# The last chunk's blocks finished by VectorE's add and a plain store, a plain matmul for the biases, one more tile added in chunk 2

## The chip, the cores and the metric

The kernel runs on one core of a Trainium2 chip. The metric is device time in microseconds; before the change it is 209.16 (median of three runs, 208.89 to 209.57). One execution was profiled.

## The reference

One layer with two branches on the same normalized input, 2048 rows of 640, bf16:

```python
x = A_x
xn = _layernorm(x, axis=-1)
return x + _A_ref(xn, A_wqkv, A_wo) + _B_ref(xn, B_w1, B_b1, B_w2, B_b2)

# branch A: 32 heads of 20; row s attends to rows s, s-2, ..., s-14
qkv = (x @ wqkv).reshape(B, S, 3, H, Dh)            # then q, k, v by head
idx = pos[:, None] - (arange(8) * 2)[None, :]       # masked where idx < 0
logits = einsum("bhsd,bhswd->bhsw", q, kg) * scale  # kg, vg: k, v gathered at idx
o = einsum("bhsw,bhswd->bhsd", softmax(logits), vg)
A = o.reshape(B, S, D) @ wo

# branch B: a layer of 1536
B = einsum("bsf,fd->bsd", gelu(einsum("bsd,df->bsf", x, w1) + b1), w2) + b2
```

## The kernel before

The 2048 rows are cut into four chunks (0 to 3) of 512 rows, each of four blocks of 128. For a chunk: statistics and normalized rows (`st`, `su`, `sq`, `rs`, `rc`, `xn`), the transpose xnT (`tp` and `tc` on TensorE for chunk 0, a DMA transpose `tc` on the SP queue for the others), the projections q, k, v in five groups of five matmuls each (`pj`, copied from PSUM by ScalarE's `pc`; chunk 0 in halves, `hj` and `hc`), and the hidden layer in twelve groups of five (`f1`), with Gelu on ScalarE (`ge`).

The attention multiplies q by shifted k on VectorE (`qk`, into two large tiles `half[0]` and `half[1]`, four window positions each and five slices of 128 features). TensorE sums over features with a 128x32 matrix `head_of` (`lg`, line 483): per half one round of four matmuls (one for each block) for each slice. To make these fewer, VectorE first adds slices together: `pa` adds slices 1 and 3 onto 0 and 2, `pb` adds slice 2 and then 4 onto 0. `LEVEL[n]` says how far this goes in chunk n: 0 leaves five slices to TensorE, 1 leaves three, 2 two, 3 one. Then the softmax: maximum and subtraction (`m`, `mx`), exponential on ScalarE (`ex`), sums (`ss`), reciprocal on ScalarE (`ri`), product (`at`), an expansion of the weights by DMA (`xd`, `xs`, SP queue), products with v into the same `half` tiles (`av`), three adds (`ad`) and a last one into `oT` (`ot`, line 606). `oT` has one buffer for all chunks.

Output of chunks 0 to 2: for each slice s of 128 output features a PSUM tile T gathers five pieces `t{n}{s}0` to `4` (line 708): four of three matmuls over the hidden layer, and piece 4 of five matmuls over oT. ScalarE adds the bias (`u`), a DMA transpose on SP turns it back to rows (`ut`), and an accumulating DMA from POOL adds it in DRAM (`ud`) to x, which `xp` stored there earlier (SP for chunk 0, ScalarE's queue otherwise).

Output of chunk 3 is made by rows: `o3{bl}{pc}` has five pieces for each block bl, each of three (five) pairs of matmuls, `lo` for columns 0 to 511 and `hi` for 512 to 639. Blocks 12 and 13 (bl 0, 1) are copied from PSUM by ScalarE (`oc`) and accumulated by POOL (`od`) onto x (`xp3`) and the bias b2 (`xb3`, an accumulating DMA of the broadcast bias). Blocks 14 and 15 are direct: `xl` adds b2 to their x rows in SBUF, VectorE adds PSUM and x (`dc` for bl 2, `oclo` and `ochi` for bl 3, line 680) and plain stores write them (`dd`, the second half of `oclo`, `ochd`). The hi part of bl 3 comes last on TensorE (`ohi`, 17 matmuls of 128 columns). In PSUM bl 0 and the hi of bl 1 share the one place of pool psL; the hi parts of bl 2 and 3 share one place of psA.

PSUM pools: psA with four places (`pj`, `hj`, `f1`, the first transposes, and pieces of the last output), psL with one of twice the size (logits, the bias transpose, the last output), psO with two (T tiles, first transposes, lo of bl 3). A place is given again when the copy that empties it is done.

The biases b1 and b2 are loaded as 17 rows of 128 into `b_rt`; `tb` (line 460) transposes them on TensorE, in a 32x32 form, and `b1` copies them to `bT`.

The order of the work is one string, ORDER, written out by hand or by a search: the pieces are emitted in it, and each of TensorE, VectorE, ScalarE and the SP queue keeps this order as it stands; semaphores come from the data. So for each engine what stands ahead of a piece can be counted in the string.

Of the kernel before, what the change touches and what calls it, by code (L numbers as in the profile page):

```python
# [17 lines left out]
P = 128  # L18
# [11 lines left out]
LASTB = S // P - 1  # L30
DIRECT = 2
WARM = 10
RB = 32
# [3 lines left out]
LEVEL = (1, 0, 2, 3)  # L37
# [10 lines left out]
pc102 pa001 qk011 pj111 pc111 pj112 pj113 pc112 pa000 pa011 lg0 mask m0a mx0a ge0_4 pc113 ge0_10 ex0a pj103 pc103  # L48
pj104 pc104 ldx m0b mx0b ex0b ss0a ri0a pj110 pc110 ss0b ri0b pj114 pc114 pj100 pc100 ld2 pj101 at0a at0b xd0 pc101
qk110 qk100 su22 hj211 hc211 f10_1 pj121 su23 ge0_1 qk101 f10_6 qk111 ge0_6 f10_8 su21 ge0_8 su20 pc121 xs0 f10_9  # L50
# [5 lines left out]
av130 av100 t004 u00 ut00 sq31 pj200 pc200 t010 av101 t011 av120 t012 t013 t020 sq30 av131 t014 u01 ut01 sq33 f11_1  # L56
rs3 rc3 t021 t022 t023 t024 t030 t031 t032 t033 xn31 t034 tc31 ad10 pad21 xn33 tc33 ad11 pc203 ad12 ot1 ud00 f11_4
ud01 pc202 qk201 ge1_1 ge1_11 xn30 qk211 qk200 f11_8 f12_11 f12_9 qk210 pa211 tc30 pa200 pa210 xn32 tc32 pad22 ge1_8
ge2_9 pa201 f12_3 ge2_11 f11_6 ge1_6 ge1_4 f12_7 pad31 pb212 u02 pj320 pc320 ge2_7 pj304 pc304 pj311 pc311 pb202 pj313
pc313 pj312 pc312 pj222 u03 pc222 xl pj302 pc302 pj301 pj310 pj300 pc310 ge2_3 f13_2 pc300 pc301 pj314 pc314 pj322  # L60
pj303 pc303 pj321 lg2 f11_3 ge3_2 ge1_3 qk310 m2 ut02 f13_8 ge3_8 xb3 f12_5 pa301 t100 pc322 f13_6 t120 pj221 t101
t102 ge2_5 mx2 t121 f12_8 qk300 ex2 ss2 ri2 pa300 t103 pc221 ut03 ut04 ud02 at2 xd2 qk311 xs2 t104 ge2_8 f13_9 ge3_9
t122 t123 u10 f13_10 ge3_10 f13_7 ge3_7 qk301 ud03 pa311 pa310 f13_1 t110 ge3_1 ge3_6 t111 t112 t113 pj323 f12_1 pb302
pj223 pb312 pb304 pc223 pc321 ud04 pb314 t114 u11 pc323 ut10 ut11 f13_0 lg3 ud10 av200 t124 u12 t140 t141 m3 mx3 t130
t131 av210 ut12 t142 ex3 ss3 t143 pj324 av230 ri3 at3 t132 t133 t134 t144 ge3_0 av211 u13 av201 av220 f12_0 ge2_0
ge2_1 pc324 f13_4 ut13 f13_3 f12_4 av221 av231 ad20 ad21 u14 xd3 f13_5 ge2_4 ge3_3 ut14 o310 f12_6 ad22 ot2 ge3_5
ge3_4 o311 o312 ud11 ud12 ud13 ud14 f12_2 xs3 ge2_6 ge2_2 f12_10 pad32 ge2_10 o320 t210 t211 t212 t200 t201 t202
f13_11 ge3_11 t203 t204 t213 t214 u20 ut20 ud20 u21 ut21 ud21 av311 av301 t220 t221 t222 t230 av310 av321 o321 t223
t224 u22 ut22 ud22 t231 t232 t233 t234 u23 ut23 ud23 o330 o331 t240 t241 t242 o300 o301 o313 av330 av320 av300 av331
ad31 t243 t244 u24 ut24 ud24 ad30 o322 o323 ad32 ot3 o302 o303 o314 o304 o324 o332 dc dd o333 o334 ohi oclo ochi oc31  # L70
od31 oc30 ochd od30
# [4 lines left out]
def kernel(  # L76
# [37 lines left out]
    outp = ctx.enter_context(tc.tile_pool(name="outp", bufs=2))  # L114
# [7 lines left out]
    b_rt = consts.tile([RB, P], BF16, name="b_rt")  # L122
# [335 lines left out]
    def do_tb():  # L458
        tiles["tb"] = psL.tile([P, 2 * W * P], BF16, tag="L", name="tb")
        nc.tensor.transpose(tiles["tb"][:, 0:RB], b_rt[:], ident[0:RB, 0:RB])  # L460

    def do_b1():
        nc.vector.tensor_copy(bT[:], tiles["tb"][:, 0 : FT + KT])
# [171 lines left out]
    def out_ps(bl, hi):  # L635
        first = lambda: psL.tile([P, W, P], F32, tag="L", name="tail")
        if bl == 0 or (hi and bl == 1):
            ps = get("tail", first)[:].rearrange("p w c -> p (w c)")
            return ps[:, CH + bl * P : CH + (bl + 1) * P] if hi else ps[:, 0:CH]
        key = "hi" if hi else ("lo", bl)  # L640
        pool, tag = (psO, "o") if key == ("lo", BPC - 1) else (psA, "acc")
        ps = get(key, lambda: pool.tile([P, CH], F32, tag=tag, name="hi" if hi else "lo"))
        return ps[:, (bl - BPC + DIRECT) * P : (bl - BPC + DIRECT + 1) * P] if hi else ps[:]

    opened = set()

    def do_o(bl, pc, parts):
        n, cs = NCH - 1, slice(bl * P, (bl + 1) * P)
        if pc < 4:
            srcs = [(tiles["hT", n, ft][:, cs], w2_sb[:, ft, :]) for ft in range(3 * pc, 3 * pc + 3)]  # L650
        else:
            srcs = [(tiles["oT", n][:, t, cs], wo2[:, t, :]) for t in range(KT)]
        for k, (lhs, rhs) in enumerate(srcs):
            final = pc == 4 and k == len(srcs) - 1
            if "lo" in parts:
                nc.tensor.matmul(out_ps(bl, False), lhsT=lhs, rhs=rhs[:, 0:CH], start=pc == 0 and k == 0, stop=final)  # L656
            if "hi" in parts:
                bank = bl // 2
                first = bank not in opened
                opened.add(bank)  # L660
                nc.tensor.matmul(
                    out_ps(bl, True), lhsT=lhs, rhs=rhs[:, CH:D], start=first, stop=final, skip_group_check=True
                )
# [11 lines left out]
    def direct(bl, hi):  # L675

        b = (NCH - 1) * BPC + bl
        room = half[1][:].rearrange("p w t c -> p (w t c)")[:, (bl % 2) * D : (bl % 2 + 1) * D]
        cs = slice(CH, D) if hi else slice(0, CH)
        nc.vector.tensor_tensor(out=room[:, cs], in0=out_ps(bl, hi), in1=x_sb[:, b, cs], op=ALU.add)  # L680
        return room, out_sd[b * P : (b + 1) * P, :]
# [70 lines left out]
    for name in "tb b1 mean1 ho ldx ld2 ldo xl dc dd oclo ohi ochi ochd mask pk".split():  # L752
        piece(name, locals()[f"do_{name}"])
# [130 lines left out]
```

## Time and profile before

| | us |
|---|---|
| median of three runs | 209.16 (208.89 to 209.57) |
| the profiled execution, its time | 209.39 |
| its span | 207.2 |
| TensorE's last matmul ends | 203.8 |
| the last store lands | 205.99 |
| DMA transposes of xnT, issue to landing | 2.4 in the median, 5.7 at most |
| accumulating stores out_dram<-x_sb, issue to landing | 3.8 in the median |
| last stores out_dram<-half: 160 KB, 128 KB, 32 KB, issue to landing | 4.2, 2.2, 1.8 |

PE is TensorE, DVE VectorE, ACT ScalarE, SP the queue of the sync engine, POOL GpSimd. A timeline line has start and length, engine, line of the code, operation, output and input, shapes, count, and in brackets the idle time just before it and what ended it. Matmuls are pipelined: a row's length is that of one matmul from entry to exit, while the next one starts sooner. "Busy" of a group is the union of these lengths.

### The profile page before, as it was taken

Reading aid. Unit: us, or ns where it says so; the run is one execution under the profiler, and the core shown is the slowest. Engines: PE = TensorE matmul, PEld = TensorE weight load, DVE = VectorE, ACT = ScalarE, POOL = GpSimd, SP = SyncE. Lnnn points to the kernel's source line nnn. Section 1 sums busy time; section 2 is a strip of 40 time slices with the busy share of each in tenths; the row PEclk is TensorE's granted clock in tenths of the full one; section 3 lists DMA queues with packets and bytes.
Section 4 is the critical chain, followed back from the end, with each engine's and each line's share of the span. In section 5 each row is a group of like instructions: output and inputs, shape, how many; then the busy total and the mean of one; then the engine's idle time right before and its main releaser. Section 6 shows DMA issues by size and latency. Waiting matters only on the chain.

```text
span 207.2 us, 2936 instructions
## 1 busy us (share of the span) xinstructions
PE 201.7 (97%) x1137; PEld 106.8 (52%) x1156; DVE 182.6 (88%) x155; ACT 126.4 (61%) x232; POOL 23.9 (12%) x36
## 2 busy tenths in 40 slices
PE   8999999999999999999999999999999999999993
PEld 3999654644444555444455544444444444444552
DVE  2889994799799899999999989999899999999611
ACT  5778967999879877658685537571658621220120
POOL 2000000000000000420002400002040220224050
PEclk9999999999999999999999999999999999999999
DMA  6995879186063358479324800073472970285455
GB/s 211 389 395 180 60 209 394 39 187 209 0 186 67 130 118 211 103 99 86 69 27 52 75 3 0 0 156 73 53 69 45 157 110 3 51 76 51 54 37 115
DMA packets 36607, 23.56 MB, mean 114 GB/s; under 512 B 24946, under 2 KB 34418, under 8 KB 36594
## 3 DMA queue, kind: packets, MB, share of 16 engines
q1 hardware_dynamic: 26464, 18.91, 36.2%
q0 software_dynamic: 8480, 2.62, 16.5%
q10 hardware_dynamic: 1650, 1.84, 2.5%
q8 instruction: 9, 0.15, 0.3%
q14 instruction: 4, 0.03, 0.1%
HBM read 10.00 MB, written 5.24 MB: 74 GB/s over the span
## 4 chain that ended last, share of the span: by engine, by line
PE 68%; DVE 14%; ACT 8%; DMA 6%; issue 1%; SPq 0%; DVEq 0%; ACTq 0%
PE T L708 18%; PE hps L613 15%; PE pps L340 15%; DVE half L592 10%; PE gps L384 6%; PE lo L656 5%; DMA x_sb<-attn 3%; DMA xnT<-xn 3%; PE idle L450 2%; ACT hT L629 2%; PE tail L656 2%; PE L L483 1%; ACT trash L222 1%; PE gps L353 1%; DVE half L601 1%
## 5 line engine op out<-in xcount | busy, mean ns | idle before, releaser
L613 PE MATMUL hps<-xnT,w_sb 128*128 128x512 bf16 x236 | 55.5, 379 | 0.4 <-ACT hT L629 0.2
L437 DVE TENSOR_TENSOR half<-qT,kT 128x5120 bf16<-128x5120 bf16 x16 | 44.4, 2820 | 2.0 <-PE L L483 1.0
L708 PE MATMUL T<-hT,w_sb 128*128 128x512 bf16 x173 | 41.9, 379 | 0.4 <-issue 0.2
L613 PEld LDWEIGHTS <-w_sb 128*128 128x128 bf16 x240 | 23.3, 98 | 27.9 <-issue 0.9
L720 POOL DMA_DIRECT2D out_dram<-x_sb x15 | 19.3, 1286 | 92.2 <-DMA x_sb<-x_sb 91.5
L629 ACT ACTIVATE hT<-hps,bT 128x512 bf16<-128x512 f32 x36 | 23.8, 689 | 9.0 <-PE hps L613 9.0
L708 PEld LDWEIGHTS <-w_sb 128*128 128x128 bf16 x180 | 17.4, 98 | 21.0 <-issue 0.4
L592 DVE TENSOR_TENSOR half<-vT,ax 128x2560 bf16<-128x2560 bf16 x16 | 23.0, 1484 | 2.5 <-ACT vT L404 2.5
L711 ACT ACTIVATE x_sb<-T,bT 128x512 bf16<-128x512 f32 x15 | 10.3, 690 | 20.9 <-PE T L708 20.9
L592 DVE TENSOR_TENSOR half<-vT,x_sb 128x2560 bf16<-128x2560 bf16 x16 | 22.6, 1485 | 0.2 <-DMA x_sb<-attn 0.2
L601 DVE TENSOR_TENSOR half<-half,half 128x5120 bf16<-128x5120 bf16 x8 | 22.3, 2820 | 0.1
L340 PE MATMUL pps<-xnT,wv_sb 128*128 128x512 bf16 x73 | 18.4, 379 | 0.1
L708 PE MATMUL T<-oT,wo 128*128 128x512 bf16 x75 | 18.3, 379 | 0.0
L340 PE MATMUL pps<-xnT,wq_sb 128*128 128x512 bf16 x74 | 17.8, 379 | 0.1
L340 PE MATMUL pps<-xnT,wk_sb 128*128 128x512 bf16 x72 | 17.5, 379 | 0.2
L174 ACT ACT_TABLE_LOAD x12 | 15.4, 1283 | 0.9 <-PEq L868 0.7
L469 DVE TENSOR_TENSOR half<-half 128x2048 bf16<-128x2048 bf16 x12 | 14.1, 1218 | 0.0
L264 ACT ACTIVATE xn<-x_sb,nmr,rstd 128x640 bf16<-128x640 bf16 x12 | 11.0, 921 | 4.1 <-DVE nmr L254 2.8
L340 PEld LDWEIGHTS <-wv_sb 128*128 128x128 bf16 x75 | 8.8, 117 | 7.6
L340 PEld LDWEIGHTS <-wq_sb 128*128 128x128 bf16 x75 | 8.7, 118 | 7.6 <-issue 0.6
L340 PEld LDWEIGHTS <-wk_sb 128*128 128x128 bf16 x75 | 8.8, 117 | 7.4
L404 ACT CAST kT<-pps 128x512 bf16<-128x512 f32 x15 | 8.7, 581 | 6.1 <-PE pps L340 6.1
(104 smaller groups left out, 239.1 us busy)
## 6 DMA issues: line engine op xcount, KB each, us to landing
w_sb<-in_B_w_dram SPq DMA_DIRECT2D x4, 960.0 KB, 10.2
ax<-attn SPq DMA_DIRECT2D x8, 256.0 KB, 4.8
x_sb<-attn SPq DMA_DIRECT2D x8, 256.0 KB, 4.6
out_dram<-x_sb POOLq DMA_DIRECT2D x15, 128.0 KB, 3.8
x_sb<-in_A_x_dram SPq DMA_DIRECT2D x1, 1280.0 KB, 7.6
out_dram<-x_sb ACTq DMA_DIRECT2D x2, 640.0 KB, 5.3
wq_sb<-in_A_wqkv_dram SPq DMA_DIRECT2D x1, 800.0 KB, 4.8
wk_sb<-in_A_wqkv_dram SPq DMA_DIRECT2D x1, 800.0 KB, 6.9
```

Source lines behind the costliest of these rows:

```text
L174: nc.scalar.preload_act_table_set(name)
L340: nc.tensor.matmul(ps[:], lhsT=wqkv_p[which][:, ti, to, :], rhs=xnT[:, ti, :], start=(ti == 0), stop=(ti == KT - 1),)
L384: nc.tensor.matmul(ps[:, to - a, :], lhsT=wqkv_p[which][:, ti, to, :], rhs=tiles["xnT", 0][:, ti, pair * 2 * P : (pair + 1) * 2 * P], star ...
L437: nc.vector.tensor_tensor(out=half[h][:, :, :, cs], in0=q[:, :, at].unsqueeze(1).to_broadcast([P, W // 2, KT, 2 * P]), in1=window(k, h, at ...
L469: nc.vector.tensor_tensor(out=even, in0=even, in1=odd, op=ALU.add)
L592: nc.vector.tensor_tensor(out=half[h][:, :, :, cs], in0=window(qkv_tile(n, 2), h, cs), in1=ax_view(n)[:, j, ws, :].unsqueeze(2).to_broadca ...
L601: nc.vector.tensor_tensor(out=a, in0=a, in1=b, op=ALU.add)
L613: nc.tensor.matmul(ps[:], lhsT=w1_sb[:, ti, ft * P : (ft + 1) * P], rhs=tiles["xnT", n][:, ti, :], start=(ti == 0), stop=(ti == KT - 1),)
L629: nc.scalar.activation(hT, tiles["hps", n, ft][:], ACT.Gelu_apprx_tanh, bias=bT[:, ft : ft + 1], scale=1.0)
L656: nc.tensor.matmul(out_ps(bl, False), lhsT=lhs, rhs=rhs[:, 0:CH], start=pc == 0 and k == 0, stop=final)
L708: nc.tensor.matmul(ps[:], lhsT=lhs, rhs=rhs, start=pc == 0 and k == 0, stop=pc == 4 and k == len(srcs) - 1)
L720: nc.gpsimd.dma_start(dst, src, accum_op=ALU.add)
```

## The change

All four blocks of chunk 3 are finished as blocks 14 and 15 were: VectorE adds PSUM and x + b2 (`dl` for lo, `dh` for hi, into places of their own in `half[1]`), then a plain store (`dd0` to `dd2` of 160 KB and `dlo` on SP, `dhi` on ScalarE's queue). `xl` is split in two pairs of blocks (`xl0`, `xl1`), both behind `ot3`. `xp3`, `xb3`, `oc` and `od` are gone. Each block and each part has a PSUM place of its own: bl 0 in psL, bl 1 and 2 in psA, bl 3 in psO. The biases come by a plain 128x128 matmul of 17 columns. LEVEL of chunk 2 goes from 2 to 3: `pb2*4` adds one more tile for each half, and `lg2` has 8 matmuls where it had 16. ORDER is new as a whole; of it the start, the stretches around lg1 and around the first use of oT of chunk 0, and the end are shown.

```diff
-LEVEL = (1, 0, 2, 3)
+LEVEL = (1, 0, 3, 3)
 ORDER = """
-tp01a gb3 tp01b tc01a tc01b gb4 gd gc0 ge tb hj100 st02a st02 rs02 st03a gc1 st03 rs03 xn02 tp02 gc4 ho b1 xn03 st11a
-st13a st10a st12a st10 hc100 st11 hj102 tp03 st13 tc02 tc03 st12 hj101 hc101 hj110 hc110 hc102 hj010 pk rs1 rc1 hj012
-hc012 xn12 tc12 hj112 hc112 hj011 hj111 hc010 qk000 xn10 tc10 hc111 hj210 hc210 hc011 hj200 qk001 hc200 xn11 tc11
-hj212 hc212 qk010 pad11 hj202 f10_5 hj201 f10_10 xn13 hc202 hc201 f10_4 f10_0 ge0_5 f10_7 ge0_0 tc13 pj102 pa010 ge0_7
...
-f10_2 f11_7 ge0_9 ge0_2 ng2 ge1_7 f10_3 f11_9 pj124 lg1 av030 av000 ldo t040 av001 sq23 sq22 ge0_3 sq21 pc124 sq20 rs2
-rc2 av031 av010 m1 f11_2 xp1 av011 av021 av020 mx1 ad00 t000 t041 xn22 tc22 pj123 pc123 xn23 tc23 f11_0 ge1_0 ge1_2
-t042 xn21 tc21 f10_11 ge0_11 xn20 tc20 t001 t002 f11_5 ge1_5 pad12 ge1_9 f11_10 ge1_10 t003 ex1 ss1 pj122 f11_11 pj120
-pc120 t043 pc122 pj210 pc210 ri1 at1 pj214 pc214 ad01 xp0 xd1 pj220 pc220 pj211 pc211 xp2 su30 ad02 ot0 pj201 pc201
-pj204 pc204 su31 xs1 pj212 pc212 pj224 pj213 pc224 pj202 su32 su33 ng3 av111 pc213 pj203 sq32 t044 u04 av110 av121 xp3
...
-ad31 t243 t244 u24 ut24 ud24 ad30 o322 o323 ad32 ot3 o302 o303 o314 o304 o324 o332 dc dd o333 o334 ohi oclo ochi oc31
-od31 oc30 ochd od30
+tp01a gb3 tp01b tc01a tc01b gb4 gd gc0 ge hj101 st02a tb st03a st02 rs02 st03 ho xn02 tp02 rs03 xn03 b1 st10a st12a
+st11a st13a st12 st13 gc4 gc1 tc02 tp03 tc03 hj100 hc100 hj102 st11 hc101 hc102 pk hj010 hc010 hj112 st10 rs1 hc112
+rc1 xn12 qk000 xn10 hj111 hc111 tc12 tc10 hj011 hc011 hj201 hc201 hj110 hj012 qk001 hc012 hc110 qk010 xn11 tc11 xn13
+pa000 hj210 hj202 hc202 hj200 tc13 hc210 ldx ld2 ldo hc200 f10_0 f10_7 ge0_7 f10_10 f10_4 pj113 ge0_4 ge0_0 pj112
...
+ge1_5 sq23 ge0_5 f11_10 hj211 hc211 f10_3 pj121 lg1 av020 xp0 ge1_10 m1 sq21 ge0_3 av000 pj120 sq22 sq20 rs2 rc2 t040
+t041 mx1 pc120 av010 xn22 av001 pc121 xn23 ex1 t000 pj123 tc22 av021 tc23 av031 av011 av030 ss1 f10_11 pj122 pc122
+ad00 t001 f10_8 ge0_8 xn21 tc21 f11_9 ge0_11 xn20 tc20 pc123 t002 f11_2 xp1 t042 t043 f11_7 ge1_2 ge1_7 f11_8 ge1_9
+ri1 at1 xp2 pad12 ad01 ad02 ot0 pj124 pc124 t003 pj211 pc211 su33 pj223 pc223 pj212 pj202 pc212 xd1 av111 su30 pj201
+av110 pc201 av100 av101 pc202 su32 pj214 pc214 pj224 xs1 av121 av120 av131 pc224 av130 pj204 pc204 pj203 t004 su31
...
+t241 t242 t243 t244 u24 o330 o331 o332 o333 ad31 o323 ad32 ot3 o324 o314 o304 xl0 o334 ohi xl1 dl2 ud14 dh2 dl1 dh1
+dl0 dh0 ut24 ud23 dl3 dd1 dd2 dd0 dlo dh3 ud24 dhi
 """.split()
...
-    def do_xl():
-        rows_ = x_sb[:, LASTB + 1 - DIRECT :, :]
+    def do_xl(pair):
+        rows_ = x_sb[:, (NCH - 1) * BPC + 2 * pair : (NCH - 1) * BPC + 2 * pair + 2, :]
...
     def do_tb():
-        tiles["tb"] = psL.tile([P, 2 * W * P], BF16, tag="L", name="tb")
-        nc.tensor.transpose(tiles["tb"][:, 0:RB], b_rt[:], ident[0:RB, 0:RB])
+        tiles["tb"] = psL.tile([P, W, P], F32, tag="L", name="tb")
+        nc.tensor.matmul(tiles["tb"][:, 0, 0 : FT + KT], lhsT=b_rt[:], rhs=ident[:, 0 : FT + KT], start=True, stop=True)
...
     def out_ps(bl, hi):
-        first = lambda: psL.tile([P, W, P], F32, tag="L", name="tail")
-        if bl == 0 or (hi and bl == 1):
-            ps = get("tail", first)[:].rearrange("p w c -> p (w c)")
-            return ps[:, CH + bl * P : CH + (bl + 1) * P] if hi else ps[:, 0:CH]
...
+        if bl == 0:
+            both = get("first", lambda: psL.tile([P, W, P], F32, tag="L", name="both"))[:].rearrange("p w c -> p (w c)")
+            return both[:, CH:D] if hi else both[:, 0:CH]
+        pool, tag = (psO, "o") if bl == BPC - 1 else (psA, "acc")
+        ps = get(("out", bl, hi), lambda: pool.tile([P, CH], F32, tag=tag, name="hi" if hi else "lo"))
+        return ps[:, 0 : D - CH] if hi else ps[:]
...
-    def do_oc(bl):
-        osb = outp.tile([P, D], BF16, tag="osb", name="osb")
-        tiles["osb", bl] = osb
-        nc.scalar.copy(osb[:, 0:CH], out_ps(bl, False))
-        nc.scalar.copy(osb[:, CH:D], out_ps(bl, True))
-
-    def do_od(bl):
+    def do_dc(bl, hi):
+
+        b, cs = (NCH - 1) * BPC + bl, slice(CH, D) if hi else slice(0, CH)
+        room = half[1][:].rearrange("p w t c -> p (w t c)")[:, bl * D : (bl + 1) * D]
+        nc.vector.tensor_tensor(out=room[:, cs], in0=out_ps(bl, hi), in1=x_sb[:, b, cs], op=ALU.add)
+
+    def do_dd(bl, cs, eng):
         b = (NCH - 1) * BPC + bl
-        nc.gpsimd.dma_start(out_sd[b * P : (b + 1) * P, :], tiles["osb", bl][:], accum_op=ALU.add)
...
+        room = half[1][:].rearrange("p w t c -> p (w t c)")[:, bl * D : (bl + 1) * D]
+        eng.dma_start(out_sd[b * P : (b + 1) * P, cs], room[:, cs])
...
+            piece(f"dl{bl}", do_dc, bl, False)
+            piece(f"dh{bl}", do_dc, bl, True)
+            if bl < last:
+                piece(f"dd{bl}", do_dd, bl, slice(0, D), nc.sync)
+        piece("dlo", do_dd, last, slice(0, CH), nc.sync)
+        piece("dhi", do_dd, last, slice(CH, D), nc.scalar)
```

More of the change, by code (lines that the diff above doesn't have):

```diff
@@ L58 @@
[L58 to L67, printed above, removed]
@@ new lines @@
+pb202 t102 pb212 pb204 pb214 lg2 ut02 f13_7 pc304 pc301 qk300 ge3_7 ut03 f11_11 m2 pa300 ge1_11 mx2 f13_1 ge3_1 t103
+t104 u10 ex2 qk311 ss2 ri2 pa311 f13_10 t120 t121 at2 pj221 pc221 f13_8 ge3_4 qk310 t122 t123 t124 t140 t141 t142
+ge3_8 f12_7 u12 pj321 pc321 pj324 pc324 xs2 xd2 ge3_10 qk301 ut04 ut10 pj220 t110 t143 f13_0 ge3_0 t111 f12_5 pj323
+ge2_5 f12_10 pc220 ud02 pc323 pa301 pa310 pb302 pb312 pb304 pb314 f13_5 lg3 ge2_10 av220 ud10 f13_11 pad32 ge3_11
+ge3_5 m3 mx3 t112 t113 t114 av210 ex3 t144 ss3 u11 av230 f12_0 ut11 ut12 ri3 at3 av201 f13_9 av231 av200 f12_2 t130
@@ L121 @@
     wo2 = wts.tile([P, KT, D], BF16, name="wo2")
-    b_rt = consts.tile([RB, P], BF16, name="b_rt")
+    b_rt = consts.tile([P, P], BF16, name="b_rt")
     nc.gpsimd.memset(b_rt[:], 0.0)
@@ L302, in do_xp @@
         (nc.scalar if n else nc.sync).dma_start(dst, x_sb[:, cs, :])
-    def do_xb(n):
-        cs, dst = rows(n)
-        nc.gpsimd.dma_start(dst, b2bc[:].unsqueeze(1).to_broadcast([P, cs.stop - cs.start, D]), accum_op=ALU.add)
-    def do_xl():
-        rows_ = x_sb[:, LASTB + 1 - DIRECT :, :]
+    def do_xl(pair):
+        rows_ = x_sb[:, (NCH - 1) * BPC + 2 * pair : (NCH - 1) * BPC + 2 * pair + 2, :]
         nc.vector.tensor_tensor(
-            out=rows_, in0=rows_, in1=b2bc[:].unsqueeze(1).to_broadcast([P, DIRECT, D]), op=ALU.add
+            out=rows_, in0=rows_, in1=b2bc[:].unsqueeze(1).to_broadcast([P, 2, D]), op=ALU.add
         )
@@ L653, in do_o @@
         for k, (lhs, rhs) in enumerate(srcs):
[L654 to L662, printed above, removed]
-                )
-    def do_oc(bl):
-        osb = outp.tile([P, D], BF16, tag="osb", name="osb")
-        tiles["osb", bl] = osb
-        nc.scalar.copy(osb[:, 0:CH], out_ps(bl, False))
-        nc.scalar.copy(osb[:, CH:D], out_ps(bl, True))
-    def do_od(bl):
-        b = (NCH - 1) * BPC + bl
-        nc.gpsimd.dma_start(out_sd[b * P : (b + 1) * P, :], tiles["osb", bl][:], accum_op=ALU.add)
[L675 to L681, printed above, removed]
+            for hi in parts:
+                nc.tensor.matmul(
+                    out_ps(bl, hi),
+                    lhsT=lhs,
+                    rhs=rhs[:, CH:D] if hi else rhs[:, 0:CH],
+                    start=pc == 0 and k == 0,
+                    stop=pc == 4 and k == len(srcs) - 1,
+                )
+    def do_dc(bl, hi):
[3 more added lines that the diff above has]
+    def do_dd(bl, cs, eng):
+        b = (NCH - 1) * BPC + bl
+        room = half[1][:].rearrange("p w t c -> p (w t c)")[:, bl * D : (bl + 1) * D]
+        eng.dma_start(out_sd[b * P : (b + 1) * P, cs], room[:, cs])
     def spent_x(i):
@@ L750, in piece @@
         pieces[name] = lambda: fn(*args)
-    for name in "tb b1 mean1 ho ldx ld2 ldo xl dc dd oclo ohi ochi ochd mask pk".split():
+    for name in "tb b1 mean1 ho ldx ld2 ldo ohi mask pk".split():
         piece(name, locals()[f"do_{name}"])
@@ L837 @@
             continue
[L838 removed]
+        last = BPC - 1
+        for pair in range(2):
+            piece(f"xl{pair}", do_xl, pair)
         for bl in range(BPC):
             for pc in range(5):
[L841 to L844 removed]
+                piece(f"o{n}{bl}{pc}", do_o, bl, pc, (False,) if bl == last else (False, True))
+            piece(f"dl{bl}", do_dc, bl, False)
[4 more added lines that the diff above has]
+        piece("dhi", do_dd, last, slice(CH, D), nc.scalar)
     engines = {getattr(mybir.EngineType, e) for e in ("PE", "DVE", "Activation", "SP")}
```

56 lines of the change are left out of this document (17 added, 39 removed).

## The prediction

> **What bounds the kernel.** I read the page's busy table and its 40 slices first, then the timelines of TensorE (PE) and VectorE (DVE), then the last transfers. All times are us from the span's start.
>
> ```profile
> PE 201.7 (97%) x1137; PEld 106.8 (52%) x1156; DVE 182.6 (88%) x155; ACT 126.4 (61%) x232; POOL 23.9 (12%) x36
> PE   8999999999999999999999999999999999999993
> DVE  2889994799799899999999989999899999999611
> PEclk9999999999999999999999999999999999999999
> ```
>
> TensorE is never idle: every slice but the first and last is a 9, at full granted clock. Matmuls overlap (a row says 379 ns, but 512 columns start every 0.216, 128 columns every 0.055), so I count starts. Holes of one start exist about every 10.8 us where a record is missing; I find no other gap of over 0.2 after 10. So TensorE's work sets the end; no engine's saving counts but its own, and any lateness that reaches it is paid in full. These lines carry the steps:
>
> ```profile
> 9.40 0.18 PE L460 MATMUL tb<-ident,b_rt 32*128 32x32 bf16 x1
> 9.51 1.29 PE L384 MATMUL gps<-xnT,wk_sb 128*128 128x256 bf16 x10
> 52.36 2.34 PE L483 MATMUL L<-half,head_of 128*32 128x512 bf16 x40
> 53.73 4.29 DVE L592 TENSOR_TENSOR half<-vT,ax 128x2560 bf16<-128x2560 bf16 x3 [1.50 <-ACT vT L404]
> 72.21 1.23 DVE L558 TENSOR_TENSOR attn<-e,rs 128x1024 bf16<-128x1024 bf16 x1 [0.71 <-ACT rs L553]
> 79.06 1.49 DVE L606 TENSOR_TENSOR oT<-half 128x2560 bf16<-128x2560 bf16 x1
> 81.41 2.32 PE L708 MATMUL T<-oT,wo 128*128 128x512 bf16 x10
> 120.93 1.05 PE L483 MATMUL L<-half,head_of 128*32 128x512 bf16 x16
> 121.91 1.47 PE L613 MATMUL hps<-xnT,w_sb 128*128 128x512 bf16 x6
> 147.05 0.62 PE L483 MATMUL L<-half,head_of 128*32 128x512 bf16 x8
> 147.60 1.25 PE L708 MATMUL T<-oT,wo 128*128 128x512 bf16 x5
> 193.58 1.49 DVE L606 TENSOR_TENSOR oT<-half 128x2560 bf16<-128x2560 bf16 x1
> 202.89 0.69 DVE L680 TENSOR_TENSOR half<-lo,x_sb 128x512 bf16<-128x512 f32 x1 [1.54 <-PE lo L656]
> 203.84 0.29 DVE L680 TENSOR_TENSOR half<-hi,x_sb 128x128 bf16<-128x128 f32 x1 [0.26 <-PE hi L661]
> ```
>
> The reader sees the bias transpose between two TensorE runs; the logits of chunks 1, 2 and 3 (40, 16 and 8 matmuls); oT of chunk 0 ending at 80.55 and its first user at 81.41; oT of chunk 3 ending at 195.07, while TensorE works on to 203.64 (the last start 0.055 before); and VectorE starting 0.2 after the matmuls it waits for.
>
> **The change, part by part.**
>
> Logits of chunk 2: 8 matmuls fewer. 16 hold TensorE from 120.93 to 121.91, 0.98; 8 hold it from 147.05 to 147.60, 0.55. So -0.43, with nothing to cover, as TensorE has no gaps. VectorE pays two more pb adds of 1.16 each (the row of four in chunk 3 takes 4.62): +2.3. xl (0.82) leaves the middle of its queue, so 1.5 more lies ahead of ot3. It costs nothing while VectorE stays ahead of TensorE; checked below.
>
> Bias matmul: the 30 matmuls before it start from 7.63 at 0.055, so end at 9.29; the next run starts at 9.51. The transpose holds TensorE 0.22. A 128x128 matmul of 17 columns isn't in the trace: between 0 and the 0.055 of 128 columns, and I take 0.05, so 0.17 saved. The Trainium skill (TensorEngine Tiling (Array Packing), Instruction Overhead) gives a matmul some 60 cycles however few its columns; at 2.4 GHz that is an estimated 0.025, and the saving would be 0.195. But the new start can give it back: tp03 and hj100 take the psA places that the copies gc4 and gc1 free, and these now stand behind rs03 on ScalarE. rs03's input is there at 9.7, so gc4 ends near 10.6 and gc1 near 11.1 (rows of 0.35 and 0.59), where TensorE wants hj100 near 10.9. I take -0.10, bounds -0.22 and +0.2.
>
> Last chunk: gone are xp3 and xb3 (stores on ScalarE's queue and POOL's), four ScalarE copies (0.59, 0.59, 0.27, 0.28) and POOL's two accumulating stores (0.89, 1.23): none on TensorE's path, so nothing gained. TensorE's matmuls here are the same number and shape. VectorE gains two adds for each of blocks 0 and 1 (0.69 and 0.28) and has two xl of 0.82 behind ot3. xl0 and xl1 (1.64) run beside o324 (5 times 0.272, 1.36), which dl2 waits for anyway; then each block costs VectorE 0.97 against 1.36 on TensorE, so it keeps up. dl0 and dh0 run from 1.83 to 0.86 before TensorE's end; dl3 can start 0.75 before it, as oclo does now (202.89 against 203.64). Then dh3 and dhi follow as today: 0.
>
> Last stores: today dhi's like lands at 205.99, 2.35 behind TensorE's end. dd0 is issued about 0.8 before that end, so it may take 3.15 to land. No such store without accumulating ones beside it is in the trace; the nearest are the 128 KB store of 2.2 and the 160 KB store of 4.2, in whose time both accumulating stores were landing (to 203.28 and 205.38). Those are gone, so I take the first: 0, with +1.0 as the far end. The Trainium skill (DMA: Bandwidth & Descriptors, Anatomy of one DMA) has about 2.0 us plus bytes/436e3, an estimated 2.4 for 160 KB; the trace agrees for the 128 KB store (2.3 against 2.2), not for the other, and by it too the term would be 0.
>
> The new order: does anything reach TensorE late? I compared what stands ahead of each meeting point in both orders, at 1.08 for a group of five 512-column matmuls and 0.65 for three, and shifted the times of before by the difference, behind lg2 by its -0.43 too. Ahead of lg0 TensorE has half a group less, so it comes at 31.93; VectorE's work ahead is the same and ended at 31.38. Ahead of lg1 one group less: 51.28; VectorE loses half a us of waiting for lg0 and most of the 0.97 before chunk 1's products, and ends near 50.8. It restarts 1.37 behind lg1, as now: 52.65, so 1.08 earlier. at1's wait of 0.71 goes, since the sums ss1 now stand before ad00 (2.74 of cover for the reciprocal); ot0 ends at 80.55-1.08-0.71=78.76. Its first user, t004, has two groups less ahead: 79.25. Margin 0.5, where it is 0.86 now. From ot0 to chunk 2's last add VectorE needs 39.3 as now plus 2.3: 120.4, for lg2 at 121.80. Chunk 3's last add: 147.2, for lg3 at 147.91. ot2: 173.80+0.86=174.66, for t204 at 175.16. ot3: 195.93, for o324 at 197.10 (o332 and o333, 1.29, more ahead than o314 has now). Margins 1.4, 0.7, 0.5 and 1.17. Psum places: ScalarE's copies, set against an unstalled TensorE, free each place at least 0.3 ahead in both orders. I allow 0.10 for the thin ones, bounds 0 and +1.4 (first rival).
>
> Sum: -0.43-0.10+0+0+0.10 = -0.43. The profiled execution took 209.39 (span 207.2 and 2.2 around it), so 208.96; it lies 0.23 above the median of 209.16, so 208.73.
>
> **Rivals.**
>
> 1. oT of chunk 0 comes late (the slower side). Its user moves forward 2.16 while VectorE's work ahead is unchanged, so all hangs on VectorE waiting less. If its waits stay as in before, ot0 ends at 80.55 and t004, wanting it at 79.25, stands 1.3, and all of TensorE behind it: 208.73+1.3=210.0. Speaking for it: the wait named at 72.21 is on ScalarE, where ri1 now stands behind ge1_2 to ge1_9 and their table load (1.28). Against: lg1, which sets the restart, comes earlier by a count of matmuls. It stalls from an ot0 behind 79.2, and is slower than before by 0.3% from 80.3.
>
> 2. The x transposes of chunk 1 land late. The fourth, issued at 23.40, landed at 27.84 (4.4, against 2.4 for the median), with the 1280 KB load of x right behind it on SP; its user started at 28.05. Now xn13 is some 0.9 earlier (three hc copies and a pad less ahead, one more), the user pj113 1.62 earlier, at 26.43. With 4.4 again it lands at 26.9: +0.5, 209.2. With 2.4 there is no stall.
>
> 3. The thin margins all hold and the start gives nothing back: -0.43-0.22, and the last landing 0.1 to 0.2 shorter without accumulating stores beside it: 208.3.
>
> 4. dd0 lands as slowly as the 160 KB row, after dhi: +1.0, 209.7.
>
> **Chances.** Forecast 0.33, rival 1 0.25, rival 2 0.15, rival 3 0.22, rival 4 0.05. A measurement of this kernel tells from no change about 0.3%, which is 0.63 us: faster is below 208.53, slower above 209.79. The forecast (its own range 208.4 to 209.0) gives 0.08 to faster and 0.25 to within; rivals 2 and 4 are within, 3 faster, 1 slower: 0.30, 0.45, 0.25. Predicted 208.7; the range, 208.1 to 210.3, reaches from rival 3 past rival 1 by the sizes I am unsure of.
>
> **What would show it.** lg2 with 8 matmuls in 0.55; no gap of 0.1 around tb; TensorE's first T<-oT of chunk 0 near 79.2 straight behind other matmuls, with oT ended before it (rival 1: a gap there, released by VectorE's L606 line); the first pps of chunk 1 near 26.4 (rival 2: a gap released by the xnT transpose); ot3 ended a us before its first user; the last out<-half landing being dhi's (rival 4: dd0's). Wrong altogether if TensorE shows gaps of over 1 us elsewhere, or its count of matmul starts is not 8 lower.

## The result, and the profile after

In 20 runs of each on one chip the changed kernel takes 208.29 us in the median (208.03 to 209.09) and the kernel before 208.97 (208.61 to 209.64): the ratio is 0.9972, 95% interval 0.9962 to 0.9981. So it is 0.68 us faster, where 0.43 was forecast; by the prediction's own bounds 208.29 counts as faster, to which it gave 0.30 against 0.45 for no change. In some executions below, the clock granted to TensorE is about 1% lower and the time 1 to 2% longer; the ratios leave out those over 1.5% above the kernel's fastest, the medians do not. 0.19 of the distance between 208.29 and the forecast 208.73 is that the kernel before itself came out at 208.97 here, not at the 209.16 of the three runs that I started from.

The profiled execution took 208.24, with a span of 206.1. The page's busy table:

```profile
PE 201.9 (98%) x1148; PEld 106.2 (52%) x1148; DVE 187.1 (91%) x162; ACT 125.0 (61%) x228; POOL 20.9 (10%) x33
```

TensorE is as full as before, with 8 weight loads fewer (1156 to 1148); VectorE has 4.5 us more. TensorE's timeline at the points that the prediction named (start, length, engine, line, operation, output and input, shapes, count):

```profile
9.41 1.25 PE L376 MATMUL gps<-xnT,wk_sb 128*128 128x256 bf16 x10
10.50 0.17 PE L452 MATMUL tb<-ident,b_rt 128*128 128x17 bf16 x1
10.53 0.83 PE L277 MATMUL tp<-ident,xn 128*128 128x128 bf16 x10
...
26.43 1.89 PE L332 MATMUL pps<-xnT,wk_sb 128*128 128x512 bf16 x8
...
79.27 1.03 PE L687 MATMUL T<-oT,wo 128*128 128x512 bf16 x4
...
121.45 0.61 PE L475 MATMUL L<-half,head_of 128*32 128x512 bf16 x8
122.00 0.61 PE L605 MATMUL hps<-xnT,w_sb 128*128 128x512 bf16 x2
```

The bias matmul holds TensorE 0.03, but the ten transposes behind it take 0.83 where ten in a row take 0.73 (shown below in the run with the old bias transpose): a wait of 0.10 for xn03. The first projection of chunk 1 starts at 26.43, oT of chunk 0 is first used at 79.27, lg2 holds TensorE from 121.45 to 122.00, 0.55. VectorE's timeline, with the idle time ahead in brackets:

```profile
77.17 1.49 DVE L598 TENSOR_TENSOR oT<-half 128x2560 bf16<-128x2560 bf16 x1
...
121.94 2.83 DVE L429 TENSOR_TENSOR half<-qT,kT 128x5120 bf16<-128x5120 bf16 x1 [1.99 <-PE L L475]
...
194.11 1.49 DVE L598 TENSOR_TENSOR oT<-half 128x2560 bf16<-128x2560 bf16 x1
195.52 1.55 DVE L302 TENSOR_TENSOR x_sb<-x_sb,b2bc 128x1280 bf16<-128x1280 bf16 x2
198.26 0.69 DVE L655 TENSOR_TENSOR half<-lo,x_sb 128x512 bf16<-128x512 f32 x1 [1.20 <-PE lo L643]
...
203.06 0.29 DVE L655 TENSOR_TENSOR half<-hi,x_sb 128x128 bf16<-128x128 f32 x1 [0.26 <-PE hi L643]
```

oT of chunk 0 ends at 78.66, 0.61 ahead of its user; VectorE waits 1.99 for lg2; behind ot3 it waits for TensorE before every pair of adds, so the direct finish never holds anything. Of the stores, as the view of the DMA issues lists them (KB each, median us to landing):

```profile
out_dram<-half SPq DMA_DIRECT2D x3, 160.0 KB, 1.8
out_dram<-half SPq DMA_DIRECT2D x1, 128.0 KB, 1.7
out_dram<-half ACTq DMA_DIRECT2D x1, 32.0 KB, 1.5
```

In this pair of profiles TensorE's last start is 0.77 earlier (203.58 to 202.81), and the last store lands 2.03 behind TensorE's end, not 2.35. lg2 explains 0.43 of the 0.77. The bias is worth some 0.1, but this execution loses 0.11 at 7.16, where a transpose of chunk 0 waits for its normalized rows. What is left stands at one place of the kernel before, where I had read a hole (a distance between two starts that is longer than a matmul needs) as a missing record:

```profile
97.81 3.40 PE L613 MATMUL hps<-xnT,w_sb 128*128 128x512 bf16 x14
101.41 2.75 PE L613 MATMUL hps<-xnT,w_sb 128*128 128x512 bf16 x12 [0.20 <-ACT hT L629]
```

A missing record leaves a hole of exactly one start: this stretch has one too, at 98.03, of 0.216 and with no releaser named (a releaser is what ended the wait), and so counts 14 rows where three groups of five stand. At 100.83 the two starts are 0.58 apart, 0.365 more than a start, and a releaser is named; the row's 0.20 is less because it lets the matmul before run to its modelled end. ScalarE's timeline says what was late:

```profile
98.91 1.73 ACT L264 ACTIVATE xn<-x_sb,nmr,rstd 128x640 bf16<-128x640 bf16 x2 [1.29 <-DMA xnT<-xn]
100.55 0.23 ACT L413 COPY vT<-vT 128x70 bf16<-128x70 bf16 x1
```

The third normalized block of chunk 3 waits 1.29 for the buffer that the DMA transpose tc31 reads. tc31 took 5.67 (93.16 to 98.83), and for most of it the accumulating store ud01 ran (92.46 to 97.08). The pad of v (100.55) and then Gelu stand behind it on ScalarE, and f11_6 behind the PSUM place that Gelu empties. The changed kernel has no such gap.

### The profile page after: what moved, and what is told of

It reads as the page before. It is cut to its first block, busy times and chain, and to the rows that moved or that the text cites. A ratio compares the mean times of both kernels' runs of the same rounds, so it can differ in the third digit from the quotient of the medians.

```text
span 206.1 us, 2934 instructions
## 1 busy us (share of the span) xinstructions
PE 201.9 (98%) x1148; PEld 106.2 (52%) x1148; DVE 187.1 (91%) x162; ACT 125.0 (61%) x228; POOL 20.9 (10%) x33
## 4 chain that ended last, share of the span: by engine, by line
PE 96%; DMA 1%; ACT 1%; DVE 0%; issue 0%
PE T L687 27%; PE hps L605 25%; PE pps L332 24%; PE gps L376 7%; PE lo L643 5%; PE L L475 2%; PE both L643 2%; PE gps L345 1%; PE hi L643 1%; DMA x_sb<-in_A_x_dram 1%; PE tp L277 1%; ACT trash L218 0%; DVE xn L262 0%; ACT logv L242 0%; DVE half L655 0%; ACT rstd L245 0%
## 5 line engine op out<-in xcount | busy, mean ns | idle before, releaser
L687 PE MATMUL T<-hT,w_sb 128*128 128x512 bf16 x180 | 43.4, 379 | 0.0
L332 PE MATMUL pps<-xnT,wk_sb 128*128 128x512 bf16 x75 | 18.1, 379 | 0.0
L396 ACT CAST qT<-pps 128x512 bf16<-128x512 f32 x15 | 8.4, 582 | 7.4 <-PE pps L332 7.4
L396 ACT CAST vT<-pps 128x512 bf16<-128x512 f32 x15 | 8.6, 582 | 6.2 <-PE pps L332 6.1
```

The costliest lines, as they stand in the source:

```text
L332: nc.tensor.matmul(ps[:], lhsT=wqkv_p[which][:, ti, to, :], rhs=xnT[:, ti, :], start=(ti == 0), stop=(ti == KT - 1),)
L396: nc.scalar.copy(dest[:, to, off : off + CH], tiles["pps", n, which, to][:])
L687: nc.tensor.matmul(ps[:], lhsT=lhs, rhs=rhs, start=pc == 0 and k == 0, stop=pc == 4 and k == len(srcs) - 1)
```

## The experiments

All are compared by TensorE's own path: its last start less the start of its first projection (which waits for the weights wq or, where these land early, for the transposed rows), so that when the weights land drops out; and by how long after TensorE's end the last store lands (the last start plus 0.055). Medians and ratios are against the kernel before on the same chip.

| run | median us | ratio, 95% | weights land | TensorE's path | last store behind |
|---|---|---|---|---|---|
| before (first profile) | 209.16 | | 5.96 | 197.36 | 2.35 |
| before, once more | 208.76 | 1.0004 (0.9983 to 1.0025) | 5.72 | 197.11 | 2.01 |
| old order, later store | 208.69 | 0.9995 (0.9973 to 1.0016) | 6.01 | 197.05 | 2.00 |
| old order, 8 matmuls | 210.30 | 1.0074 (1.0045 to 1.0103) | 7.06 | 198.66 | 2.12 |
| changed (first profile) | 208.29 | 0.9972 (0.9962 to 0.9981) | 6.01 | 196.59 | 2.03 |
| changed, once more | 208.37 | 0.9972 (0.9941 to 1.0003) | 6.13 | 196.51 | 2.03 |
| changed, a third time | 208.10 | 0.9961 (0.9942 to 0.9980) | 5.86 | 196.49 | 2.03 |
| changed, lg2 of 16 | 209.31 | 0.9997 (0.9968 to 1.0026) | 7.24 | 196.94 | 2.02 |
| changed, accumulating finish | 209.91 | 1.0037 (1.0013 to 1.0062) | 7.12 | 196.51 | 3.24 |
| new order alone | 210.11 | 1.0073 (1.0043 to 1.0103) | 6.07 | 197.14 | 3.37 |
| changed, VectorE delayed | 209.33 | 1.0004 (0.9975 to 1.0032) | 6.00 | 198.14 | 2.02 |
| changed, old bias | 208.25 | 0.9959 (0.9933 to 0.9984) | 5.88 | 196.84 | 2.03 |
| one more level | 208.70 | 0.9969 (0.9936 to 1.0002) | 7.34 | 197.33 | 2.03 |
| one more level, mended | 207.58 | 0.9953 (0.9922 to 0.9985) | 8.10 | 197.75 | 2.03 |

**The eight matmuls of lg2.**

```diff
-LEVEL = (1, 0, 3, 3)
+LEVEL = (1, 0, 2, 3)
-pb202 t102 pb212 pb204 pb214 lg2 ut02 f13_7 ...
+pb202 t102 pb212 lg2 ut02 f13_7 ...
```

> The changed kernel with chunk 2's last adds (pb204, pb214) taken out again, so that lg2 has 16 matmuls. Theory (TensorE has no gaps, so every matmul start is paid): lg2 holds TensorE 0.98 in place of 0.55, its last matmul ends 0.43 later than 202.87, at 203.3, and the time is 0.43 over the changed kernel's, ratio to the kernel before 0.999. Rival (the gain came from elsewhere, the matmuls overlapped other waits): TensorE's end stays within 0.1 of 202.87 and the ratio at 0.997; then a gap stands somewhere behind lg2 that takes up the 0.43.

```profile
122.44 1.05 PE L475 MATMUL L<-half,head_of 128*32 128x512 bf16 x16
123.42 0.82 PE L605 MATMUL hps<-xnT,w_sb 128*128 128x512 bf16 x3
```

From the projections to lg2 every start lies 0.99 behind the changed kernel's, behind lg2 1.42: 0.43, and nothing takes it back. The absolute 203.3 was missed because the weights landed 1.2 later in this execution; the median and its interval are too wide to tell. The term stands by the trace.

**The finish of blocks 12 and 13, and the order alone.** The first kernel puts back ScalarE's copies and POOL's accumulating stores (and, earlier, xp3 and xb3); the second has lg2 of 16 and the old bias transpose too, so only the order and the PSUM places are new.

```diff
...
-... xl0 o334 ohi xl1 dl2 ud14 dh2 dl1 dh1 dl0 dh0 ut24 ud23 dl3 dd1 dd2 dd0 dlo dh3 ud24 dhi
+... o334 ohi xl1 dl2 ud14 dh2 ut24 ud23 ud24 oc31 od31 oc30 dl3 dd2 dlo dh3 dhi od30
...
```

> The changed kernel with blocks 12 and 13 finished in the old way: copies on ScalarE, accumulating stores from POOL, x and b2 put into DRAM earlier; blocks 14 and 15 stay direct, PSUM places and the order of TensorE stay. Theory (a plain store lands later when accumulating stores land beside it): TensorE's end stays at 202.9; the last plain store lands 2.3 to 2.4 behind it in place of 2.03, the 128 KB store takes 2.2 in place of 1.7; time +0.3, ratio to the kernel before 0.9985, more if an accumulating store lands last. Rival (the shorter landing was chance of one profile): landing 2.0 behind TensorE's end and ratio 0.997.

> The new order alone: lg2 with 16 matmuls, the old 32x32 bias transpose, and blocks 12 and 13 finished in the old way, all in the changed kernel's order. Theory (the old order had a true stall of TensorE of 0.36 at 100.8, which the new one has not): no gap of TensorE behind 11, its last matmul ends 0.3 to 0.4 before the 203.64 of the kernel before, at 203.25 to 203.35, ratio to the kernel before 0.998 to 0.9985. Rival (the hole at 100.8 was a missing record, as I predicted): TensorE ends at 203.6 to 203.7 and the ratio is 1.000.

The stores of the first of the two:

```profile
out_dram<-osb POOLq DMA_DIRECT2D x2, 160.0 KB, 3.5
out_dram<-half SPq DMA_DIRECT2D x1, 160.0 KB, 2.6
...
out_dram<-half SPq DMA_DIRECT2D x1, 128.0 KB, 3.1
out_dram<-half ACTq DMA_DIRECT2D x1, 32.0 KB, 2.7
```

TensorE's path is the changed kernel's (196.51), but the last store lands 3.24 behind its end: +1.2, four times what I expected. In the new order blocks 13 and 12 end just ahead of block 15, so the later of their accumulating stores is issued at 202.95, 0.8 before TensorE's end, and not at 200.08, 3.2 before it, as in the second profile of before; it lands at 206.60, and the plain stores issued behind it at 206.78 and 206.97. The order alone gains nothing: TensorE's last matmul ended where I expected it (203.3), but its path of 197.14 is that of before (197.11), and with the old finish the kernel is slower by 0.43 to 1.03%. The old gap is not there, but TensorE waits 0.09 at 9.30 for the weights wk, which landed at 9.25 here and at 8.88 to 9.07 in the three profiles of the changed kernel. So order and finish belong together: in the new order the direct finish avoids 1.2. No run has the direct finish of blocks 12 and 13 in the old order; the last store lands 2.35, 2.01, 2.00 and 2.12 behind TensorE's end in the four profiles there, against 2.03, so it would shorten 0 to 0.3.

**The gap at 100.8.**

```diff
-... u01 ut01 sq33 ... ud00 f11_4 ud01 pc202 ... xn32 tc32 pad22
+... u01 sq33 ... ud00 f11_4 pc202 ... xn32 tc32 ut01 ud01 pad22
```

> The kernel before with one edit in its order: the second slice's transpose back and its accumulating store of chunk 0 (ut01, ud01) are issued behind chunk 3's four xnT transposes, not ahead of them. Theory (the accumulating store of 92.5 to 97.1 made tc31 land after 5.7 and tc33 after 5.0, so that xn30, Gelu's copies behind it and so a hidden group of TensorE came late at 100.8): tc31 and tc33 land in 2.4 to 3.2, ScalarE's xn waits less than 0.3 near 98, TensorE's gap at 100.8 is gone, its end 203.25 to 203.35, ratio 0.9983. First rival (the hole is a missing record): TensorE's end stays at 203.6 and the ratio at 1.000. Second rival (something else makes the transposes slow): they land after 5 again, the gap stays.

```profile
97.18 1.97 ACT L264 ACTIVATE xn<-x_sb,nmr,rstd 128x640 bf16<-128x640 bf16 x2
```

The wait ahead of xn is gone, tc31 lands in 2.4 and tc33 in 4.0, and TensorE has no gap there. In before ut01 had landed (92.18) when tc31 was issued, so of the two things moved the store is the one that ran beside it. It is not the whole cause of late transposes: tc33 took 4.96 beside it, and still 4.0 with no such store. TensorE's path is 0.31 shorter than in the first profile of before. Yet the times are those of before (0.9973 to 1.0016), so I profiled the kernel before again, unedited.

> The kernel before, unedited, with a profile of its own. The run with the later store lost the gap of 0.36 at 100.8 in its profile, yet its times and those of the kernel before next to it were alike. Theory (the gap belongs to the one execution that was profiled: the transposes of chunk 3 land late in some executions only): here tc31 and tc33 land in under 4, no gap of TensorE at 100.8, its last start at 203.2 to 203.3 if the weights land at 6.0, the last store 2.0 behind TensorE's end; span near 206.5 and time near 208.6. Rival (the gap is the order's, in every execution): the gap stands at 100.8 again, tc31 takes over 5, last start at 203.6.

Both expectations are half right. The transposes land late in this execution too (tc31 5.48, tc33 4.75, beside the same store):

```profile
98.56 1.73 ACT L264 ACTIVATE xn<-x_sb,nmr,rstd 128x640 bf16<-128x640 bf16 x2 [1.10 <-DMA xnT<-xn]
```

but 0.2 less late, and TensorE's gap is 0.09, not 0.365. In the run with 8 matmuls in the old order, which is unchanged up to there, it is 0.53 by the starts:

```profile
102.49 3.40 PE L614 MATMUL hps<-xnT,w_sb 128*128 128x512 bf16 x15 [0.37 <-ACT hT L630]
```

So the lateness stands in all three profiles that have this stretch of the old order, and how much of it reaches TensorE differs: 0.09, 0.365, 0.53. The first profile of before was also 0.34 longer behind TensorE's end than the second (2.35 against 2.01). So the execution that the prediction read was long in two places; the 0.23 that it took off led to the median of three, itself 0.19 above that of twenty.

**The changed kernel again, twice.** No edit.

> The changed kernel once more, unedited, so that the other runs of this chip can be set against it. Theory (the 1.0 by which TensorE started late in the profile of the kernel with 16 matmuls, and the 0.9 in that of the accumulating one, lie in when the first weights land, not in the edits): from TensorE's first projection on, every start lies a constant distance (0 to 1.0) behind the first profile of the changed kernel, with no gap behind 11; ratio to the kernel before 0.996 to 0.998. Rival (the late starts came from the edits): this run's first projection starts at 6.2 again, as in the first profile, and its last matmul ends at 202.9.

> The changed kernel beside the kernel before and the last try on one chip. Theory: ratio to the kernel before 0.997 as before, TensorE's last start 196.6 behind its first projection whatever the weights' landing; the last store 2.0 behind TensorE's end. Rival: a gap of over 0.2 on TensorE behind 11 in this execution, so that the changed kernel too depends on the execution.

The paths are 196.51 and 196.49 with no gap behind 11, against 196.59, which holds the 0.11 lost at 7.16. Both executions began early (first projection at 6.18 and 6.12), so they do not themselves tell late weights from the edits; what speaks for the weights is that in the runs with 16 matmuls and with the accumulating finish the first projection is released by the landing of wq (7.24 and 7.12), ahead of all that the edits touch. From the second profile of before to the third of the changed kernel TensorE's path is 0.62 shorter, and 0.68 is what the medians of this last chip differ by (208.78 to 208.10). That the two lie so near is partly chance: the spans of these runs differ by 0.75 in the median (206.7 to 205.95), and the time outside the span went the other way.

**oT of chunk 0, my rival's place.**

```diff
+def do_dly():
+    for _ in range(4):
+        nc.vector.bn_stats(spare[:], x_sb[:, NCH * BPC - 1, 0 : D // 2])
...
-ad00 t001 ...
+dly ad00 t001 ...
```

> The changed kernel with four statistics instructions of 0.43 more on VectorE right ahead of chunk 1's first add (ad00 of chunk 0), 1.72 in all, whose results nobody reads. Theory (my first rival's place and price: oT of chunk 0 ends 0.6 ahead of its first user t004, and from there on each us of lateness is TensorE's): a gap of 1.1 on TensorE ahead of t004, released by VectorE's last add; no second gap behind it, since lg2 then comes 1.1 later too and has a margin of 1.5; TensorE's end +1.1, time +1.1, ratio to the changed kernel 1.005. Rival (other slack takes it up: the at1 wait or ScalarE's reciprocal): ot0 ends less than 79.3 and the time is unchanged.

```profile
77.19 2.32 PE L332 MATMUL pps<-xnT,wq_sb 128*128 128x512 bf16 x10
80.78 2.32 PE L693 MATMUL T<-oT,wo 128*128 128x512 bf16 x10 [1.26 <-DVE oT L604]
```

The place is right, and released by the line that I named: the starts show a gap of 1.43, and it is the only one (the row counts 1.26, since it lets the matmul before run to its modelled end). The four instructions delayed the add behind them by 1.99, not 1.72 (0.5 each in a row); 1.99 less 1.43 is a margin of 0.56. The medians differ by 0.96 (209.33 against 208.37 beside it), less than the gap, and the expected ratio of 1.005 was met by chance: the spans differ by 1.35 in the median (207.55 against 206.2), but the time outside the span is 1.75 in this kernel and 2.14 in the changed one. Why that part differs is open.

**The bias matmul.**

```diff
...
-nc.tensor.matmul(tiles["tb"][:, 0, 0 : FT + KT], lhsT=b_rt[:], rhs=ident[:, 0 : FT + KT], start=True, stop=True)
+nc.tensor.transpose(tiles["tb"][:, 0:RB], b_rt[:], ident[0:RB, 0:RB])
...
```

> The changed kernel with the old bias transpose (32x32, 17 rows) in the new order. Theory (the plain matmul saves 0.17 on TensorE, but 0.10 of it was given back as a wait of the next transposes for the normalized rows xn03, which ScalarE's rs03 sets): the tb row holds TensorE 0.2, the gap of 0.10 ahead of tp03 shrinks to nothing, and TensorE comes to its next projection 0.0 to 0.1 later; time the same within 0.1, ratio to the changed kernel 1.000. Rival (all of the 0.17 counts, as in my sum's far bound): 0.17 later from there on.

```profile
10.71 0.18 PE L453 MATMUL tb<-ident,b_rt 32*128 32x32 bf16 x1
10.82 0.73 PE L278 MATMUL tp<-ident,xn 128*128 128x128 bf16 x10
```

The ten transposes take 0.73 with no wait, so the 0.10 of waiting is filled by the slower form. Before tb the starts lie 0.12 behind the changed kernel's, behind the transposes 0.21: the plain matmul is worth 0.09. The other 0.17 by which the path is longer than in the first profile of the changed kernel stands ahead of tb: here the first six matmuls start 0.107 apart in place of 0.055. No median can tell this (208.25 against 208.37).

**The eight matmuls in the old order.**

```diff
-LEVEL = (1, 0, 2, 3)
+LEVEL = (1, 0, 3, 3)
-... pb202 pj313
+... pb202 pb214 pb204 pj313
```

> The kernel before with one edit: chunk 2's two more adds (pb204, pb214) and so 8 matmuls in lg2, in the old order. Theory (the 0.43 is to be had only if VectorE is ahead): VectorE's adds end at 119.9+2.33=122.2, lg2 was started at 120.6 to 120.9, so TensorE stands 1.4 to 1.7 ahead of it, and of that 0.43 is won back: TensorE's end and the time 1.0 to 1.3 later than the kernel before, ratio 1.005 to 1.006. Rival (what VectorE adds is hidden in its wait for lg2, in the old order as in the new): ratio 0.998.

```profile
120.83 1.24 PE L341 MATMUL pps<-xnT,wv_sb 128*128 128x512 bf16 x5
123.40 0.61 PE L484 MATMUL L<-half,head_of 128*32 128x512 bf16 x8 [1.32 <-DVE half L475]
```

TensorE stands 1.39 for VectorE's adds. The path is 1.55 longer than in the second profile of before: 1.39, less 0.43, plus 0.44 more at the old gap, plus 0.15 near 135. The saving is the order's to give: in the new one VectorE's adds end 1.5 ahead of lg2, which stands behind more TensorE work and without `xl` ahead of it.

**One more level, in chunk 0.** TensorE's matmuls are the bound and VectorE waits at each logits, so I took 8 more matmuls from TensorE.

```diff
-LEVEL = (1, 0, 3, 3)
+LEVEL = (2, 0, 3, 3)
-... pa011 lg0 mask m0a mx0a pad11 pc103 su22 ex0a pj100 pc100 pj102 pc102 m0b ...
+pa011 pb002 pb012 pad11 pc103 su22 pj100 pc100 pj102 pc102 lg0 mask m0a mx0a ex0a pj114 pc114 pj101 pc101 m0b
...
```

> A try at a faster kernel: chunk 0's logits too get two more adds on VectorE (pb002, pb012, 1.22 each), so lg0 has 16 matmuls in place of 24, and the order is changed so that lg0, lg1, t004, lg2, lg3 and t204 stand one or two groups of TensorE later, where VectorE can meet them. Theory (TensorE pays each matmul, VectorE has waits of 1.4 to 2.3 at each logits): lg0 holds TensorE 0.43 less, no gap of over 0.1 behind it, TensorE's end 0.43 earlier than the changed kernel's beside it, ratio to that 0.998. Rival (VectorE's 2.4 more come out at one of the meeting points whose margins I left at 0.1 to 0.5, likeliest lg1, lg2 or t004): a gap of 0.3 to 1 there takes it all back, ratio 1.000 or above.

The rival's result, at other places than it named: every meeting point with VectorE held. TensorE stood 0.63, 0.13 and 0.53 for Gelu (at 43.8, 46.1 and 65.0), which the first and the last time stood behind a table load of 1.28; the first:

```profile
42.12 1.24 PE L607 MATMUL hps<-xnT,w_sb 128*128 128x512 bf16 x5
43.83 4.39 PE L607 MATMUL hps<-xnT,w_sb 128*128 128x512 bf16 x19 [0.47 <-ACT hT L623]
```

```profile
41.52 0.26 ACT L547 ACTIVATE rs<-half 128x64 f32<-128x64 f32 x1
41.80 1.28 ACT L172 ACT_TABLE_LOAD   x1
43.09 0.69 ACT L623 ACTIVATE hT<-hps,bT 128x512 bf16<-128x512 f32 x1
```

The softmax's reciprocal had moved back, and the table load with it, into the time in which the hidden groups fill all four PSUM places.

```diff
-... xd0 qk100 qk101 qk110 f10_2 ge0_2 f10_9 hj212 su23 hc212 f10_1 qk111 su20 ge0_1 f11_0 ge0_9 ...
+... xd0 qk100 qk101 qk110 hj212 pj121 f10_2 f10_9 hc212 f10_1 qk111 pc121 f11_0 ge0_2 su23 ge0_1 ge0_9 ...
-... f10_11 pj122 pc122 ex1 ... tc20 pc123 t002 f11_2 ...
+... f10_11 pj122 pc123 pc122 ex1 ... tc20 f11_2 t002 ...
```

> The try with one more level in chunk 0, mended: there VectorE met all points, but TensorE stood 0.66 at 43.8 (a hidden group whose PSUM place Gelu had not emptied, behind its table load) and 0.54 near 65 (the output's second piece, whose Gelu stood behind ex1 and another table load). Now a projection group and a part of v (pj121, hj212) stand ahead of the first hidden groups, and f11_2 ahead of t002. Theory (only these two held it): no gap of over 0.1 behind 11, TensorE 0.43 ahead of the changed kernel counted from its first projection, ratio to the changed kernel beside it 0.998. Rival (a further place or VectorE's lg2, with a margin of 0.1, holds it): gaps of 0.3 or more, ratio 1.000 or above.

All three waits are gone; the largest left behind 14.3 are 0.12 for Gelu at 55.96, just ahead of lg1 and more than the 0.1 that I had allowed, and 0.07 near 74.7. The median is 207.58, against 208.10 of the changed kernel on that chip: 0.52 lower, and its eight lowest runs (207.33 to 207.73) lie below that kernel's lowest (207.98). The two intervals overlap, so the size is open; TensorE's saving by count is 0.43, less these two waits. About half of the 0.52 is not TensorE's: the spans differ by 0.25 in the median (205.95 to 205.7), and the rest is time outside the span, 1.8 in place of 2.1 for a reason that no run shows. Its path in the table is no measure: in the profiled execution TensorE's granted clock was 0.75 from 6 to 12. From 14.3 on TensorE gains 0.28 on the first profile of the changed kernel.

## Why the prediction was near, and where it was wrong

**lg2: -0.43.** Measured 0.43, in both directions of the edit (0.55 against 0.98, and 0.43 lost with 16).

**Bias: -0.10.** Measured -0.09. That the size agrees is partly luck, for I had the give-back in the wrong place: not gc4 and gc1 made hj100 late, but tp03 waited 0.10 for xn03, behind rs03.

**Last chunk: 0, last stores: 0.** Against the second profile of before right: 2.01 and 2.03 behind TensorE's end. That the direct finish gains nothing is wrong for this order, where it avoids 1.2; I priced it apart from the order. The far end of +1.0 was far too high: 160 KB lands in 1.8 without accumulating stores issued beside it. My third rival's 0.1 to 0.2 from the last landing appears only against the first profile.

**New order: +0.10.** Measured -0.09 against the second profile of before, -0.365 against the first: the old gap, which the new order does not have. The step that failed is the sentence that I find no other gap of over 0.2 after 10 and that the holes are missing records. I counted holes and did not look at what stands at each: this one was longer than a start and had a releaser. So it was also wrong that ScalarE's copies free each PSUM place at least 0.3 ahead in both orders: here Gelu freed one late. The sum thus gave the new order a risk and no gain. -0.43-0.09-0.09 is -0.61, and TensorE's path shows -0.62.

**The margins.** lg0 31.92 against 31.93 forecast, lg1 51.28 and 51.28, VectorE's restart 52.64 and 52.65, ot0's end 78.66 and 78.76, t004 79.27 and 79.25, lg2 121.45 and 121.80, the difference being the gap. VectorE finished ahead of all. Counting what stands ahead of each meeting point was right within 0.1, but for that gap.

**The rivals.** The first (oT late) has its place and mechanism confirmed by the delay; its condition did not occur, since at1's wait of 0.71 went as counted. The second is wrong: the fourth transpose of chunk 1 landed in 2.5, ahead of the 26.43 that I had forecast. The fourth (dd0 slow) is wrong: dd0 landed at 203.74, before dhi at 204.89. 208.29 is the third's time, for other reasons than it gave: the start did give something back, and what it lacked was the old gap.

## What to carry to other kernels

Where one engine is full, look at every hole of its starts one by one: its length against one start and its releaser tell a missing record from a stall, and a second profile of the same kernel tells how much of it comes again. Where two kernels' times differ by a few tenths, compare the spans too: the time outside the span was 2.1 in the changed kernel and 1.75 to 1.8 in three of the runs. Price a finish and the order it stands in together: the plain stores here are worth 1.2 us in the new order and, by when the last store landed there, at most 0.3 in the old one. And when work moves from the full engine to one that waits, move the meeting points with it, and see which table loads move too.

## What was unexpected of the hardware

- **When the first weights land.** The same 800 KB load of wq, issued at 1.2, landed between 5.72 and 6.13 in nine profiled executions and at 7.06 to 8.10 in five. In the nine TensorE's first projection starts at 6.11 to 6.22, in the five at 7.11 to 8.15, and all of its work that much later. It would explain, though no run shows it, why times come in two groups: the first repeat of the changed kernel has seven runs at 207.99 to 208.44 and five at 209.14 to 209.52. Such groups hide effects of 0.4 in a median of 12 runs.
- **DMA transposes beside an accumulating store.** tc31 took 5.5 to 5.7 in three profiles, 2.4 with the store moved away. tc33 took 4.6 to 5.0 and 4.0, and the fourth transpose of chunk 1 took 4.4 in the first profile with no such store, so something else makes transposes late too; what it is no run here shows.
- **Plain stores beside accumulating ones.** Those issued while one was running landed only after it (206.78 and 206.97 behind 206.60; 204.90, 205.10 and 205.30 behind 204.73). With none running at their issue, 32, 128 and 160 KB take 1.50, 1.70 and 1.79 (dd0). The Trainium skill (DMA: Bandwidth & Descriptors, Anatomy of one DMA) has 2.0 plus bytes/436e3 for DMAs of GpSimd's queue, 2.4 for 160 KB; the slope agrees (an estimated 0.30 for 128 KB more, 0.29 measured), the fixed part is nearer 1.4 for these stores from SP and ScalarE, and the measurement decides.
- **Logits cost more than their matmuls.** Wherever nothing else holds it, each run of the 128x32 form has a gap of 0.093 before and 0.096 behind it, 0.19 of lg2's 0.55, in all fourteen profiles. The Trainium skill (TensorEngine Tiling (Array Packing), Key Properties) says that a change of the tiling mode drains TensorE; the gaps agree, and they mean that halving the matmuls of such a group saves less than half of its time.
